# Attention sums of a chunk in one run over four PSUM banks, with the Exp table loaded by its own instruction

## The chip, the cores and the metric

The kernel runs on one core of one Trainium2 chip. Times are device microseconds (us) of that core, taken in several executions ("rounds") that alternate between the compared kernels on the same chip. The span is the time from the first to the last instruction in one profiled execution, and is some 1.7 us shorter than the time. The clock of a run is the share of full speed that TensorE was granted. Of the engines, TensorE is PE in the profile (its weight loads PEld), VectorE is DVE, ScalarE is ACT. A bracket at the end of a profile line gives how long the engine stood idle before it, and what ended that.

## The reference, cut to what matters

```python
xn  = layernorm(x)                      # x: 2048 x 512
q, k, v = split(xn @ wqkv)              # 32 heads of 16
# each position attends to itself and to 7 earlier ones, 2 apart
attn = softmax(einsum("bhsd,bhswd->bhsw", q, kg) * 16**-0.5)    # masked below 0
s = einsum("bhsw,bhswd->bhsd", attn, vg) @ wo
g = silu((gelu(xn @ w_gate) * (xn @ w_up)) @ w_down)            # inner width 1792
out = x + s * g
```

## The kernel before

The 2048 positions go in four chunks of 512. A chunk runs through a gate/up stage (14 groups: a `g_ps` and a `u_ps` of four 128x512 matmuls each), the projections of the next chunk (12 groups `qkv_ps`), and the down projection (`y_ps`, `s_ps`). Between these groups the attention of the chunk is laid in: VectorE multiplies q by k (`pk`) and the weights by v (`pv`), and TensorE sums these products over the head's elements or over the window with constant matrices of 32 columns, four such matmuls side by side. A list says ahead of which group each piece of attention stands.

The program lays out eight banks of 128x512 f32 in PSUM, the memory into which TensorE writes: five for the pool `mm`, through which all groups pass, two for the tile that is logits or half the sums in turn, one for the denominators. Tiles of one tag take turns in the same banks, so a new one waits until the last reader of the old one has ended.

```python
mm = pool("mm", 5, space=PSUM)
att = pool("att", 1, space=PSUM)

def logits(j):
    L = att.tile([P, WH, TQ], F32, name="L_ps", tag="pair")
    ...                                    # 32 matmuls of 32 columns
    nc.scalar.activation(out=E[:], in_=L[:], func=AF.Exp, scale=SCALE)

def denominators(j):
    den = att.tile([P, P], F32, name="den_ps")
    ...                                    # 8 matmuls with 32 columns of weights
    nc.vector.reciprocal(out=rs[:], in_=den[:])

def av_sums(j, gg):                        # one half: 16 matmuls
    o = att.tile([P, 2, TQ], F32, name="o_ps", tag="pair")
    for g in range(2):
        for wh in range(WH):
            for i in range(4):
                nc.tensor.matmul(o[H * i : H * (i + 1), g, :], lhsT=hsum[:],
                                 rhs=st[j]["pv"][2 * gg + g, wh][:, i, :],
                                 start=(wh == 0), stop=(wh == WH - 1))

# chunk 0, among the projections of chunk 1
at(("qkv", 1, 3), denominators, 0)
at(("qkv", 1, 3), av_sums, 0, 0)
at(("qkv", 1, 5), spread_reciprocals, 0)
at(("qkv", 1, 6), divide, 0, 0)
at(("qkv", 1, 10), av_sums, 0, 1)
at(("qkv", 1, 10), divide, 0, 1)
# chunks 1 to 3, among their own gate/up groups
at(("glu", j, 7), denominators, j)
at(("glu", j, 7), av_sums, j, 0)
at(("glu", j, 9), spread_reciprocals, j)
at(("glu", j, 9), divide, j, 0)
at(("glu", j, 12), av_sums, j, 1)
at(("glu", j, 12), divide, j, 1)

qs = [mm.tile([P, HQ], F32, name="qkv_ps", tag="mm") for _ in range(NC)]   # first q groups
```

The softmax here doesn't subtract the row's maximum and nothing guards it: scores larger than these inputs give would overflow.

Of the kernel before, what the change touches and what calls it, by code (L numbers as in the profile page):

```python
# [8 lines left out]
ALU = mybir.AluOpType  # L9
AF = mybir.ActivationFunctionType  # L10
BF16 = mybir.dt.bfloat16
F32 = mybir.dt.float32

P = 128
# [5 lines left out]
WH = 2  # L20
PAD = 16
TQ = 512
VW = TQ + WL * DIL
EPS = 1e-5
SCALE = DH ** -0.5
# [3 lines left out]
def kernel(  # L29
# [13 lines left out]
    nc = tc.nc  # L43
    B, S, D = A_x.shape
    DF = B_w_gate.shape[1]
    NT, NC, NF, NJ = S // P, D // P, DF // P, S // TQ
# [6 lines left out]
    def pool(name, bufs, **kw):  # L53
        return ctx.enter_context(tc.tile_pool(name=name, bufs=bufs, **kw))
# [10 lines left out]
    op = pool("op", 1)  # L65
# [1 line left out]
    sm2 = pool("sm2", 2)  # L67
    sm4 = pool("sm4", 4)
    dram = pool("dram", 1, space=bass.MemoryType.DRAM)
    mm = pool("mm", 5, space=bass.MemoryType.PSUM)  # L70
    att = pool("att", 1, space=bass.MemoryType.PSUM)


# [2 lines left out]
    wg_sb = wts.tile([P, NC, DF], BF16, name="wg_sb")  # L76
    wu_sb = wts.tile([P, NC, DF], BF16, name="wu_sb")
# [25 lines left out]
    def load_late_weights():  # L103
# [15 lines left out]
        out=vT.rearrange("(k p) n -> p k n", p=P)[:, :, 0:PAD],  # L119
        in_=warm[:, 0 : NC * PAD].rearrange("p (k n) -> p k n", k=NC),  # L120
# [39 lines left out]
    k_sb = big.tile([P, NC, PAD + S], BF16, name="k_sb")  # L160
# [78 lines left out]
    def project(ps, w, lo, j, i0=0, n=TQ, dks=range(NC)):  # L239
        for dk in dks:  # L240
            nc.tensor.matmul(  # L241
                ps[:],
                lhsT=w[:, dk, lo : lo + P],
                rhs=xnT[j][:, dk, i0 : i0 + n],
                start=(dk == 0),
                stop=(dk == NC - 1),
            )

    st = [dict(pk={}, pv={}) for _ in range(NJ)]

    def qkv(j, fo, i0=0, n=TQ, ps=None):
        which, c = divmod(fo, NC)
        if fo == 0 and i0 == 0:
            st[j]["q"] = qp.tile([P, NC, TQ], BF16, name="q_sb")
        if ps is None:
            ps = mm.tile([P, n], F32, name="qkv_ps", tag="mm")
            project(ps, wqkv_sb, fo * P, j, i0, n)
        if which == 0:
            nc.scalar.activation(out=st[j]["q"][:, c, i0 : i0 + n], in_=ps[:], func=AF.Copy)  # L259
        elif which == 1:  # L260
            lo = PAD + j * TQ + i0
            nc.scalar.activation(out=k_sb[:, c, lo : lo + n], in_=ps[:], func=AF.Copy)  # L262
        else:
            vst = sm4.tile([P, TQ], BF16, name="vst")
            nc.scalar.activation(out=vst[:], in_=ps[:], func=AF.Copy)  # L265
            lo = PAD + j * TQ
            nc.sync.dma_start(out=vT[c * P : (c + 1) * P, lo : lo + TQ], in_=vst[:])

# [21 lines left out]
        st[j]["pk"][w] = pk  # L290

    def logits(j):
        L = att.tile([P, WH, TQ], F32, name="L_ps", tag="pair")
        for wh in range(WH):
            for c in range(NC):
                for wl in range(WL):
                    nc.tensor.matmul(  # L297
                        L[H * wl : H * (wl + 1), wh, :],
                        lhsT=dsum[:, c, :],
                        rhs=st[j]["pk"][WL * wh + wl][:, c, :],  # L300
                        start=(c == 0),
                        stop=(c == NC - 1),
                    )
        E = st[j]["E"] = ep.tile([P, WH, TQ], BF16, name="E")
        nc.scalar.activation(out=E[:], in_=L[:], func=AF.Exp, scale=SCALE)
        if j == 0:
            for w in range(1, W):
                wh, wl = divmod(w, WL)
                nc.gpsimd.memset(E[H * wl : H * (wl + 1), wh, 0 : w * DIL], 0.0)

    def denominators(j):

        E = st[j]["E"]
        den = att.tile([P, P], F32, name="den_ps")
        for wh in range(WH):
            for q in range(4):
                nc.tensor.matmul(  # L317
                    den[H * q : H * (q + 1), :],
                    lhsT=hsum[:],
                    rhs=E[:, wh, q * P : (q + 1) * P],  # L320
                    start=(wh == 0),
                    stop=(wh == WH - 1),
                )
        rs = sm2.tile([P, P], BF16, name="rs")
        with nc.allow_low_precision(reason="as the softmax of the reference"):
            nc.vector.reciprocal(out=rs[:], in_=den[:])
        st[j]["rs"] = rs
# [20 lines left out]
        )  # L348
        st[j]["pv"][g, wh] = pv

    def av_sums(j, gg):

        o = att.tile([P, 2, TQ], F32, name="o_ps", tag="pair")
        for g in range(2):
            for wh in range(WH):
                for i in range(4):
                    nc.tensor.matmul(  # L357
                        o[H * i : H * (i + 1), g, :],
                        lhsT=hsum[:],
                        rhs=st[j]["pv"][2 * gg + g, wh][:, i, :],  # L360
                        start=(wh == 0),
                        stop=(wh == WH - 1),
                    )
        st[j]["o"] = o

    def divide(j, gg):
        if gg == 0:
            st[j]["oT"] = op.tile([P, NC, TQ], BF16, name="oT")
        nc.vector.tensor_tensor(  # L369
            out=st[j]["oT"][:, 2 * gg : 2 * gg + 2, :],  # L370
            in0=st[j]["o"][:],
            in1=st[j]["rb"][:].unsqueeze(1).to_broadcast([P, 2, TQ]),
            op=ALU.mult,
        )

    def glu(j, fc):
        g_ps = mm.tile([P, TQ], F32, name="g_ps", tag="mm")
        project(g_ps, wg_sb, fc * P, j)
        u_ps = mm.tile([P, TQ], F32, name="u_ps", tag="mm")
        project(u_ps, wu_sb, fc * P, j)  # L380
        ge = sm.tile([P, TQ], BF16, name="ge")
        nc.scalar.activation(out=ge[:], in_=g_ps[:], func=AF.Gelu_apprx_tanh)  # L382
        u = sm.tile([P, TQ], BF16, name="u")
        nc.scalar.activation(out=u[:], in_=u_ps[:], func=AF.Copy)  # L384
        h = hp.tile([P, TQ], BF16, name="h")
        nc.vector.tensor_tensor(out=h[:], in0=ge[:], in1=u[:], op=ALU.mult)  # L386
        st[j][fc] = h
# [35 lines left out]
    def at(key, fn, *args):  # L423
        side.setdefault(key, []).append((fn, args))
# [15 lines left out]
    for w in range(W):  # L440
        at(("glu", 0, w), qk_product, 0, w)
    at(("glu", 0, 9), logits, 0)
    for i in range(8):
        at(("glu", 0, 12 + i) if i < 2 else ("qkv", 1, (0, 1, 3, 4, 5, 6)[i - 2]),
           av_product, 0, i // 2, i % 2)
    at(("qkv", 1, 3), denominators, 0)
    at(("qkv", 1, 3), av_sums, 0, 0)
    at(("qkv", 1, 5), spread_reciprocals, 0)
    at(("qkv", 1, 6), divide, 0, 0)
    at(("qkv", 1, 10), av_sums, 0, 1)  # L450
    at(("qkv", 1, 10), divide, 0, 1)

    for j in range(1, NJ):
        for w in range(W):
            early = j > 1 and w < 3
            at(("qkv", j, 9 + w) if early else ("down", j - 1, w // 3), qk_product, j, w)
        for i in range(TPQ):
            at(("down", j - 1, i), load_v, j, [i])
        at(("glu", j, 0), logits, j)
        for i in range(8):  # L460
            at(("glu", j, 2 + i), av_product, j, i // 2, i % 2)
        at(("glu", j, 7), denominators, j)
        at(("glu", j, 7), av_sums, j, 0)
        at(("glu", j, 9), spread_reciprocals, j)
        at(("glu", j, 9), divide, j, 0)
        at(("glu", j, 12), av_sums, j, 1)
        at(("glu", j, 12), divide, j, 1)


    HT = TPQ // 2  # L470
    HQ = HT * P
# [11 lines left out]
    first_normalize(2)  # L483
    first_normalize(3)

    qs = [mm.tile([P, HQ], F32, name="qkv_ps", tag="mm") for _ in range(NC)]
    for dks in ((0, 1), (2, 3)):
        for fo in range(NC):
            project(qs[fo], wqkv_sb, fo * P, 0, 0, HQ, dks)
    for fo in range(NC):  # L490
        qkv(0, fo, 0, HQ, qs[fo])
    transpose(HT, copy=nc.vector.tensor_copy)
    for fo in range(NC, 2 * NC):
        qkv(0, fo, 0, HQ)
        if fo == NC:
            transpose(HT + 1, copy=nc.vector.tensor_copy)
# [3 lines left out]
    for fo in range(2 * NC):  # L500
        qkv(0, fo, HQ, HQ)
# [6 lines left out]
    for j in range(NJ):  # L508
        for fc in range(NF):
            run("glu", j, fc)  # L510
            glu(j, fc)
        if j + 1 < NJ:
            for i in range(12):
                run("qkv", j + 1, i)
                qkv(j + 1, i)
        for tt in range(TPQ):
            run("down", j, tt)
            down(j, tt)
# [28 lines left out]
```

## Time and profile before

| | before |
|---|---|
| time, median (first three runs) | 232.51 us (232.31 to 232.93) |
| span of the profiled run | 230.6 us |
| TensorE busy, clock granted | 97%, 0.998 |
| VectorE, ScalarE busy | 64%, 57% |
| matmuls | 1339 |

Most of the table says one thing: TensorE never rests. A reader then has to ask how much of its time is work. The busy share does not tell, since a matmul's modelled end overlaps the next one's start (a group of four is given as 1.03 us long, and the next starts after 0.86); the distance between starts does. The prediction shows the lines.

### The profile page before, as it was taken

The page shows a single profiled execution, that of the slowest core. Times are in us where ns is not written, and L with a number is a line of the kernel's source. Part 1 is how long each engine was busy: PE and PEld are TensorE (multiplying, and loading weights), DVE is VectorE, ACT ScalarE, POOL GpSimd, SP SyncE. Part 2 cuts the span into 40 slices and gives each one's busy share as a digit, 9 for nine tenths or more (in the row PEclk, how much of TensorE's full clock was granted, in tenths as well). Part 3 has the DMA queues.
Part 4 walks back from the last instruction along what each step waited for, and adds up shares of the span by engine and source line. Part 5 has one row for each costly group of instructions (what it writes and reads, how often), then busy time and mean ns, then how long its engine had stood idle before and what let it go on. Part 6 is the DMA issues. An engine that isn't in the chain of part 4 may idle for free.

```text
span 230.6 us, 3545 instructions
## 1 busy us (share of the span) xinstructions
PE 224.8 (97%) x1339; PEld 106.3 (46%) x1339; DVE 146.9 (64%) x234; ACT 132.3 (57%) x219; POOL 22.1 (10%) x61
## 2 busy tenths in 40 slices
PE   7999999999999999999999999999999999999994
PEld 5865444444444444444444444444444444444453
DVE  5593996897795198981677149951449429864132
ACT  4779869755414865756621595656741387576211
POOL 1058943000000000130000000000000000000000
PEclk9999999999999999999999999999999999999999
DMA  6999399921378211100277611000046810000001
GB/s 166 360 375 368 104 209 207 294 73 48 100 176 196 54 23 29 26 0 0 92 171 164 141 25 31 18 11 0 27 140 158 203 30 0 0 0 4 23 23 46
DMA packets 27057, 23.71 MB, mean 103 GB/s; under 512 B 6688, under 2 KB 27040, under 8 KB 27040
## 3 DMA queue, kind: packets, MB, share of 16 engines
q1 hardware_dynamic: 27040, 23.49, 38.8%
q8 instruction: 10, 0.16, 0.3%
q14 instruction: 7, 0.06, 0.1%
HBM read 18.22 MB, written 4.21 MB: 97 GB/s over the span
## 4 chain that ended last, share of the span: by engine, by line
PE 93%; DVE 3%; DMA 2%; SPq 1%; ACT 0%; issue 0%; DVEq 0%
PE g_ps L241 21%; PE y_ps L398 21%; PE u_ps L241 20%; PE qkv_ps L241 17%; PE s_ps L408 6%; PE L_ps L297 3%; PE o_ps L357 3%; DVE pv L343 2%; DMA wqkv_sb<-in_A_wqkv_dram 2%; SPq L83 1%; PE tr L207 1%; DVE h L386 0%; PE sp_ps L332 0%; PE den_ps L317 0%; ACT ge L382 0%
## 5 line engine op out<-in xcount | busy, mean ns | idle before, releaser
L241 PE MATMUL g_ps<-xnT,wg_sb 128*128 128x512 bf16 x224 | 57.6, 379 | 0.0
L241 PE MATMUL u_ps<-xnT,wu_sb 128*128 128x512 bf16 x224 | 57.5, 379 | 0.0
L398 PE MATMUL y_ps<-wd_sb,h 128*128 128x512 bf16 (+1 forms) x238 | 51.2, 367 | 0.0
L386 DVE TENSOR_TENSOR h<-ge,u 128x512 bf16<-128x512 bf16 x56 | 23.7, 424 | 34.1 <-ACT u L384 34.0
L287 DVE TENSOR_TENSOR pk<-q_sb,k_sb 128x2048 bf16<-128x2048 bf16 x32 | 37.8, 1220 | 11.6 <-ACT k_sb L262 11.6
L241 PE MATMUL qkv_ps<-xnT,wqkv_sb 128*128 128x512 bf16 (+1 forms) x224 | 43.0, 349 | 0.5 <-DMA wqkv_sb<-in_A_wqkv_dram 0.5
L382 ACT ACTIVATE ge<-g_ps 128x512 bf16<-128x512 f32 x56 | 33.6, 600 | 14.4 <-PE g_ps L241 12.9
L384 ACT ACTIVATE u<-u_ps 128x512 bf16<-128x512 f32 x56 | 33.6, 599 | 13.9 <-PE u_ps L241 13.9
L343 DVE TENSOR_TENSOR pv<-E,v_arr 128x2048 bf16<-128x2048 bf16 x32 | 38.6, 1217 | 0.0
L405 ACT ACTIVATE sl<-y_ps 128x512 bf16<-128x512 f32 (+1 forms) x17 | 9.7, 572 | 44.0 <-PE y_ps L398 44.0
L398 PEld LDWEIGHTS <-h 128*128 128x128 bf16 x238 | 23.3, 98 | 25.3
L241 PEld LDWEIGHTS <-wu_sb 128*128 128x128 bf16 x224 | 21.9, 98 | 26.6 <-issue 0.3
L241 PEld LDWEIGHTS <-wg_sb 128*128 128x128 bf16 x224 | 20.8, 98 | 26.7 <-issue 4.2
L241 PEld LDWEIGHTS <-wqkv_sb 128*128 128x128 bf16 x224 | 21.5, 98 | 20.0 <-DMA wqkv_sb<-in_A_wqkv_dram 0.7
L416 DVE TENSOR_TENSOR m<-s_ps,sl 128x512 bf16<-128x512 f32 (+1 forms) x17 | 11.2, 657 | 26.2 <-PE s_ps L408 26.2
L408 PE MATMUL s_ps<-wo_sb,oT 128*128 128x512 bf16 (+1 forms) x68 | 16.6, 366 | 0.0
L192 POOL TENSOR_TENSOR rstd<-rstd,mhalf 128x1 f32<-128x1 f32 x12 | 8.0, 665 | 79.4 <-DVE rstd L189 77.2
L259 ACT ACTIVATE q_sb<-qkv_ps 128x512 bf16<-128x512 f32 (+1 forms) x20 | 9.9, 513 | 5.4 <-PE qkv_ps L241 5.2
L265 ACT ACTIVATE vst<-qkv_ps 128x512 bf16<-128x512 f32 x16 | 9.6, 597 | 5.6 <-PE qkv_ps L241 5.6
L262 ACT ACTIVATE k_sb<-qkv_ps 128x512 bf16<-128x512 f32 (+1 forms) x20 | 10.2, 512 | 3.6 <-PE qkv_ps L241 3.2
L369 DVE TENSOR_TENSOR oT<-o_ps,rb 128x1024 bf16<-128x1024 f32 x8 | 9.7, 1218 | 1.4 <-PE o_ps L357 1.4
L408 PEld LDWEIGHTS <-oT 128*128 128x128 bf16 x68 | 6.6, 98 | 7.2
(49 smaller groups left out, 117.6 us busy)
## 6 DMA issues: line engine op xcount, KB each, us to landing
v_arr<-vT SPq DMA_DIRECT2D x16, 520.0 KB, 5.1
vT<-vst SPq DMA_DIRECT2D x16, 128.0 KB, 1.7
out_dram<-o_t SPq DMA_DIRECT2D x15, 128.0 KB, 2.3
wg_sb<-in_B_w_gate_dram SPq DMA_DIRECT2D x2, 896.0 KB
wu_sb<-in_B_w_up_dram SPq DMA_DIRECT2D x2, 896.0 KB, 13.7
wd_sb<-in_B_w_down_dram SPq DMA_DIRECT2D x1, 1792.0 KB, 16.8
wqkv_sb<-in_A_wqkv_dram SPq DMA_DIRECT2D x3, 512.0 KB, 5.1
x_sb<-in_A_x_dram SPq DMA_DIRECT2D x3, 512.0 KB, 9.7
```

The lines of the kernel that those rows point to most:

```text
L241: nc.tensor.matmul(ps[:], lhsT=w[:, dk, lo : lo + P], rhs=xnT[j][:, dk, i0 : i0 + n], start=(dk == 0), stop=(dk == NC - 1),)
L259: nc.scalar.activation(out=st[j]["q"][:, c, i0 : i0 + n], in_=ps[:], func=AF.Copy)
L262: nc.scalar.activation(out=k_sb[:, c, lo : lo + n], in_=ps[:], func=AF.Copy)
L287: nc.vector.tensor_tensor(out=pk[:], in0=st[j]["q"][:], in1=k_sb[:, :, off : off + TQ], op=ALU.mult)
L343: nc.vector.tensor_tensor(out=pv[:], in0=st[j]["E"][:, wh, :].unsqueeze(1).to_broadcast([P, 4, TQ]), in1=st[j]["va"][:, 4 * g : 4 * g + 4, ...
L369: nc.vector.tensor_tensor(out=st[j]["oT"][:, 2 * gg : 2 * gg + 2, :], in0=st[j]["o"][:], in1=st[j]["rb"][:].unsqueeze(1).to_broadcast([P, ...
L382: nc.scalar.activation(out=ge[:], in_=g_ps[:], func=AF.Gelu_apprx_tanh)
L384: nc.scalar.activation(out=u[:], in_=u_ps[:], func=AF.Copy)
L386: nc.vector.tensor_tensor(out=h[:], in0=ge[:], in1=u[:], op=ALU.mult)
L398: nc.tensor.matmul(y[:], lhsT=st[j][fc][:, tt * P : (tt + 1) * P], rhs=wd_sb[:, fc, cols], start=(fc == 0), stop=(fc == NF - 1),)
L408: nc.tensor.matmul(s[:], lhsT=st[j]["oT"][:, g, tt * P : (tt + 1) * P], rhs=wo_sb[:, g, cols], start=(g == 0), stop=(g == NC - 1),)
L416: nc.vector.tensor_tensor(out=m[:], in0=s[:], in1=sl[:, cols], op=ALU.mult)
```

## The change

Its intent: a chunk's 32 sums in one run, so that TensorE goes to the 32-column form and back less often. This needs four banks for the sums at once, so the pool `mm` falls from five to four, and the denominators move into the pool. The other parts are to make the smaller pool bearable: the Exp table is loaded by its own instruction ahead of the logits, and the four q groups at the start use the sums' banks, idle at that time. In chunk 0, where the sums waited for VectorE, the whole run and the spread of the reciprocals stand later.

```diff
-    mm = pool("mm", 5, space=bass.MemoryType.PSUM)
+    mm = pool("mm", 4, space=bass.MemoryType.PSUM)
...
     def logits(j):
-        L = att.tile([P, WH, TQ], F32, name="L_ps", tag="pair")
+        nc.scalar.preload_act_table(AF.Exp)
+        L = att.tile([P, NC, TQ], F32, name="L_ps", tag="quad")
...
-        den = att.tile([P, P], F32, name="den_ps")
+        den = mm.tile([P, P], F32, name="den_ps", tag="mm")
...
-    def av_sums(j, gg):
+    def av_sums(j):
-        o = att.tile([P, 2, TQ], F32, name="o_ps", tag="pair")
-        for g in range(2):
+        o = att.tile([P, NC, TQ], F32, name="o_ps", tag="quad")
+        for g in range(NC):
...
-    at(("qkv", 1, 3), av_sums, 0, 0)
-    at(("qkv", 1, 5), spread_reciprocals, 0)
-    at(("qkv", 1, 6), divide, 0, 0)
-    at(("qkv", 1, 10), av_sums, 0, 1)
-    at(("qkv", 1, 10), divide, 0, 1)
+    at(("qkv", 1, 8), spread_reciprocals, 0)
+    at(("qkv", 1, 10), av_sums, 0)
+    at(("qkv", 1, 10), divide, 0)
...
-        at(("glu", j, 7), denominators, j)
-        at(("glu", j, 7), av_sums, j, 0)
-        at(("glu", j, 9), spread_reciprocals, j)
-        at(("glu", j, 9), divide, j, 0)
-        at(("glu", j, 12), av_sums, j, 1)
-        at(("glu", j, 12), divide, j, 1)
+        at(("glu", j, 11), denominators, j)
+        at(("glu", j, 11), av_sums, j)
+        at(("glu", j, 12), spread_reciprocals, j)
+        at(("glu", j, 13), divide, j)
...
-    qs = [mm.tile([P, HQ], F32, name="qkv_ps", tag="mm") for _ in range(NC)]
+    q4 = att.tile([P, NC, TQ], F32, name="q4_ps", tag="quad")
+    qs = [q4[:, fo, 0:HQ] for fo in range(NC)]
```

More of the change, by code (lines that the diff above doesn't have):

```diff
@@ L241, in project @@
             nc.tensor.matmul(
-                ps[:],
+                ps,
                 lhsT=w[:, dk, lo : lo + P],
@@ L255, in qkv @@
         if ps is None:
-            ps = mm.tile([P, n], F32, name="qkv_ps", tag="mm")
+            ps = mm.tile([P, n], F32, name="qkv_ps", tag="mm")[:]
             project(ps, wqkv_sb, fo * P, j, i0, n)
         if which == 0:
-            nc.scalar.activation(out=st[j]["q"][:, c, i0 : i0 + n], in_=ps[:], func=AF.Copy)
+            nc.scalar.activation(out=st[j]["q"][:, c, i0 : i0 + n], in_=ps, func=AF.Copy)
         elif which == 1:
             lo = PAD + j * TQ + i0
-            nc.scalar.activation(out=k_sb[:, c, lo : lo + n], in_=ps[:], func=AF.Copy)
+            nc.scalar.activation(out=k_sb[:, c, lo : lo + n], in_=ps, func=AF.Copy)
         else:
             vst = sm4.tile([P, TQ], BF16, name="vst")
-            nc.scalar.activation(out=vst[:], in_=ps[:], func=AF.Copy)
+            nc.scalar.activation(out=vst[:], in_=ps, func=AF.Copy)
             lo = PAD + j * TQ
@@ L304, in logits @@
         E = st[j]["E"] = ep.tile([P, WH, TQ], BF16, name="E")
-        nc.scalar.activation(out=E[:], in_=L[:], func=AF.Exp, scale=SCALE)
+        nc.scalar.activation(out=E[:], in_=L[:, 0:WH, :], func=AF.Exp, scale=SCALE)
         if j == 0:
@@ L359, in av_sums @@
                         lhsT=hsum[:],
-                        rhs=st[j]["pv"][2 * gg + g, wh][:, i, :],
+                        rhs=st[j]["pv"][g, wh][:, i, :],
                         start=(wh == 0),
@@ L364, in av_sums, with divide @@
         st[j]["o"] = o
-    def divide(j, gg):
-        if gg == 0:
-            st[j]["oT"] = op.tile([P, NC, TQ], BF16, name="oT")
-        nc.vector.tensor_tensor(
-            out=st[j]["oT"][:, 2 * gg : 2 * gg + 2, :],
-            in0=st[j]["o"][:],
-            in1=st[j]["rb"][:].unsqueeze(1).to_broadcast([P, 2, TQ]),
-            op=ALU.mult,
-        )
+    def divide(j):
+        oT = st[j]["oT"] = op.tile([P, NC, TQ], BF16, name="oT")
+        for g in range(0, NC, 2):
+            nc.vector.tensor_tensor(
+                out=oT[:, g : g + 2, :],
+                in0=st[j]["o"][:, g : g + 2, :],
+                in1=st[j]["rb"][:].unsqueeze(1).to_broadcast([P, 2, TQ]),
+                op=ALU.mult,
+            )
     def glu(j, fc):
         g_ps = mm.tile([P, TQ], F32, name="g_ps", tag="mm")
-        project(g_ps, wg_sb, fc * P, j)
+        project(g_ps[:], wg_sb, fc * P, j)
         u_ps = mm.tile([P, TQ], F32, name="u_ps", tag="mm")
-        project(u_ps, wu_sb, fc * P, j)
+        project(u_ps[:], wu_sb, fc * P, j)
         ge = sm.tile([P, TQ], BF16, name="ge")
```

## The prediction

> **What bounds the kernel now.** I read the page first (busy shares, then the chain that ended last), then TensorE's timeline around each place that the change touches, then the timelines of ScalarE and VectorE in the same stretches.
>
> ```profile
> span 230.6 us, 3545 instructions
> PE 224.8 (97%) x1339; PEld 106.3 (46%) x1339; DVE 146.9 (64%) x234; ACT 132.3 (57%) x219; POOL 22.1 (10%) x61
> PEclk9999999999999999999999999999999999999999
> PE 93%; DVE 3%; DMA 2%; SPq 1%; ACT 0%; issue 0%; DVEq 0%
> ```
>
> TensorE (PE) is busy 97% of the span at full clock, and 93% of the chain is its own work, so the change must save time on PE. Busy is not peak, so I take starts: four 128x512 matmuls of one group start every 0.863 us (for example u_ps at 43.85, next group at 44.71), 0.216 us each. No part of the change removes a column from PE's stream (the order of instructions has 1339 matmuls before and after), so what can be won is only what stands between the groups: mode changes and stalls.
>
> Chunk 1, the second run of the attention sums (columns: start us, us, engine, line, op, count):
>
> ```profile
> 96.79 1.03 PE L241 MATMUL u_ps<-xnT,wu_sb 128*128 128x512 bf16 x4
> 97.75 1.05 PE L357 MATMUL o_ps<-pv,hsum 128*32 128x512 bf16 x16
> 98.73 1.04 PE L241 MATMUL g_ps<-xnT,wg_sb 128*128 128x512 bf16 x4
> ```
>
> u_ps should give way at 96.79 + 0.863 = 97.65; the 32-column matmuls start at 97.75, so going in costs 0.10. They are 16, four side by side: 4 x 0.216 = 0.863, end 98.61; g_ps starts at 98.73, so coming out costs 0.11. One visit of the sums costs 0.21 us beyond its work.
>
> Chunk 0, where the sums wait for a product on VectorE:
>
> ```profile
> 44.71 2.75 PE L241 MATMUL qkv_ps<-xnT,wqkv_sb 128*128 128x512 bf16 x12
> 47.40 0.29 PE L317 MATMUL den_ps<-E,hsum 128*32 128x128 bf16 x8
> 47.52 0.82 PE L357 MATMUL o_ps<-pv,hsum 128*32 128x512 bf16 x12
> 48.61 0.40 PE L357 MATMUL o_ps<-pv,hsum 128*32 128x512 bf16 x4 [0.27 <-DVE pv L343]
> 48.94 1.90 PE L241 MATMUL qkv_ps<-xnT,wqkv_sb 128*128 128x512 bf16 x8
> ```
>
> From den_ps to the next qkv_ps 1.54 us pass. In chunk 1 the same work, without a wait, takes 1.09 (den_ps at 87.70, g_ps at 88.79). The stall is 0.45 us; the bracket shows 0.27 because modelled ends hide the rest.
>
> Chunk 2, where the Exp table is loaded only after the logits have ended:
>
> ```profile
> 130.24 1.28 ACT L305 ACT_TABLE_LOAD   x1 [2.22 <-PE L_ps L297]
> 131.54 1.02 ACT L305 ACTIVATE E<-L_ps 128x1024 bf16<-128x1024 f32 x1
> 132.58 1.28 ACT L382 ACT_TABLE_LOAD   x1
> 133.87 0.60 ACT L382 ACTIVATE ge<-g_ps 128x512 bf16<-128x512 f32 x1
> ...
> 133.49 1.03 PE L241 MATMUL g_ps<-xnT,wg_sb 128*128 128x512 bf16 x4
> 134.52 1.02 PE L241 MATMUL u_ps<-xnT,wu_sb 128*128 128x512 bf16 x4
> ```
>
> The load waited for L_ps. In chunks 0, 1 and 3 it starts before the logits end (35.01, 73.52, 182.73). In chunk 2 everything behind it on ScalarE comes some 1.2 us later, and u_ps starts at 134.52 instead of 133.49 + 0.863 = 134.35: a stall of 0.17 until ge (ends 134.47) frees a bank, with all five in use. From this I take 0.05 us from an end on ScalarE to the start on PE.
>
> **What the Trainium skill says.** "TensorEngine Tiling (Array Packing)", Key Properties, says that changing the tiling mode drains TensorE; the trace agrees that a change costs, 0.10 going in and 0.11 coming out. "ScalarE: Activation LUTs", What ACT_TABLE_LOAD costs, gives 1283 ns for a load plus about 1380 ns of drain; the trace has 1283 ns, but no such drain beside it (load over at 131.52, Exp starts at 131.54), so I count 1.28. "PSUM — Partial Sum Buffer", PSUM bank collisions, tells one to guard by bank: a group can't write a bank until its reader has left it. The 0.17 us stall above is that. This is what a pool of four banks instead of five makes more likely.
>
> **The change part by part.** The order of instructions gives the new positions and what each waits for.
>
> 1. One run of sums in chunks 1 to 3. Before: den_ps + 16 matmuls after gate/up group 6, 16 more after group 11. After: den_ps + 32 matmuls after group 10. One visit fewer in each chunk: 3 x 0.21 = -0.63 us. Does it wait for the products? In chunk 1 the last product follows the h of group 8. That h starts 1.75 us after its u_ps, then 0.34, then 1.22 for the product. Without the earlier run group 8 has ended at 87.60 + 2 x 1.73 = 91.06, its u_ps began at 90.2, and the product is done at about 93.5. The sums start at 87.60 + 4 x 1.73 + 0.10 = 94.6 and need the last product 1.6 us later still. No wait. The spread one group later needs the reciprocal (0.95), hidden behind 1.7 us of sums and 1.7 of group 11.
>
> 2. Chunk 0. den_ps stays where it is, alone; all 32 sums stand at qkv 10. Visits: two before, two after, so nothing is saved in changes of mode. But the 0.45 us wait goes: the products end on VectorE at 53.91, and PE reaches the sums at about 47.62 + 20 x 0.216 + 0.22 (spread) + 8 x 0.216 = 53.9, needing the last product at the end of a 1.7 us run. -0.45 us. den_ps holds one of the four banks until the reciprocal at about 50.6; the compiled order shows the groups after it rotating over the other three, each free well before its turn (0.86 made, 0.60 to empty). No stall.
>
> 3. Exp table by its own instruction. In chunks 0, 1, 3 nothing moves: the load is already early. In chunk 2 it loses its wait, Exp starts at 130.2, and the 0.17 us stall goes. -0.17 us. The number of table loads stays 14.
>
> 4. Four banks instead of five. I take each group's bank from the compiled program and the end of its earlier reader from the trace. After Exp in chunk 1: g_ps wants to start at 78.97, its bank is free at 78.62 + 0.05, margin 0.3; chunk 0, 39.53 against 39.29, margin 0.24. These hold only because the table is early. One place doesn't hold, at the start of chunk 0's gate/up, where transposes share the pool:
>
> ```profile
> 20.73 1.03 PE L241 MATMUL u_ps<-xnT,wu_sb 128*128 128x512 bf16 x4
> ...
> 19.00 1.28 ACT L382 ACT_TABLE_LOAD   x1
> 20.30 0.60 ACT L382 ACTIVATE ge<-g_ps 128x512 bf16<-128x512 f32 x1
> ```
>
> This u_ps now takes the bank of the g_ps whose ge ends at 20.90: it starts at 20.95 instead of 20.73. +0.22 us. The transpose and groups after it then find their banks free.
>
> 5. First q groups in the sums' banks. They hold four banks that are idle then, so that the pool of four isn't empty. The four copies are now released by the last of 16 matmuls, so they start near 8.75 instead of 8.10; the k copy behind them ends at about 10.25, its bank is wanted at 10.31. 0 to +0.05 us.
>
> 6. VectorE does the same instructions. The division now comes as two of 1.22 us together, after the whole run. In chunk 0 that puts the next products about 0.6 us later; they ended at 70.1 where the logits took them at 73.7. In chunk 3, where no projections follow: the last h starts after both divisions, ending about 5.65 us after the start of group 12's g_ps; the down projection asks for it at 3.45 + 13 x 0.216 = 6.26. It holds, with 0.6 to spare.
>
> Sum: -0.63 - 0.45 - 0.17 + 0.22 = -1.03 us. The span of 230.6 becomes about 229.6 and the time of 232.51 about **231.5 us**, 0.4% faster.
>
> **Rivals.** (a) The smaller pool becomes the limit: PE waits for ScalarE after every Exp. The margins of 0.24 and 0.3 us are thin; if release takes 0.3 us longer than I read, each chunk loses some 0.1 to 0.3, the gain is eaten: 232.0 to 232.8. For it: the bank is the only resource that shrinks. Against: PE starts 0.05 us after the release in the one stall of this kind. (b) VectorE becomes the bound at the sums or at the end, with all eight products wanted at once and two divisions in a row ahead of the last h: up to 1 us lost, 232.3. Against: the margins above, and VectorE's 64%; in chunk 1 the moments of the next tiles also queue there, so the reciprocal may come late for the spread. (c) The change of mode is cheaper to avoid than I read: if the cost lies with the shape of the next weights rather than with the visit, den_ps alone in chunk 0 could cost more, and merging save less: 231.9. (d) The waits that go are only moved: chunk 0's missing stall returns at the later sums if the products slip. Then 231.9.
>
> **Range and chances.** The terms are each known to about 0.1 us; the four rivals are worth up to 1 us, all upwards. Nothing can win 2% (4.7 us), since all mode changes and stalls together are less. Two executions of the kernel before differ by up to 0.6 us. So 230.9 to 232.3, and within 2% almost surely.
>
> **What would show each step right or wrong.** In chunks 1 to 3 den_ps and 32 o_ps in one stretch of about 1.95 us from the first den_ps to the next g_ps (0.12 + 1.73 + 0.11), with no wait for pv. In chunk 0 no bracket at o_ps for pv, and den_ps followed by qkv_ps after about 0.23 us. In chunk 2 the Exp table load ahead of the end of L_ps, and no 0.17 gap at the third u_ps. At about 20.9 a late u_ps waiting for ge. Wrong would be: gaps on PE at the third g_ps after each Exp, at the spreads, or at the 14th matmul of the first down projection of chunk 3.

## The result, and the profile after

The changed kernel takes 231.61 us (median of 6, 231.38 to 231.72) against 232.58 for the kernel before (6 runs, 232.31 to 232.93). The ratio is 0.9956, 95% interval 0.9943 to 0.9968; like all ratios here it is the mean time of one kernel's fast runs over that of the other's that were recorded with them (three of these six are the three runs above), so not quite the ratio of the medians. The change gains 0.97 us of the medians, 0.4%, where 1.0 was forecast.

The page's first lines and the shares of the chain, after:

```profile
span 229.8 us, 3547 instructions
PE 224.7 (98%) x1339; PEld 107.6 (47%) x1339; DVE 147.5 (64%) x234; ACT 132.3 (58%) x219; POOL 20.9 (9%) x61
PE 95%; ACT 1%; DVE 1%; DMA 1%; issue 0%; DVEq 0%
```

The matmuls, their busy time and, within one point, the shares of the other engines are the same; what has gone is idle time and gaps on TensorE. TensorE's timeline in chunk 1 (start us, us, engine, line, op, count):

```profile
93.64 1.03 PE L241 MATMUL u_ps<-xnT,wu_sb 128*128 128x512 bf16 x4
94.59 0.29 PE L318 MATMUL den_ps<-E,hsum 128*32 128x128 bf16 x8
94.71 1.90 PE L358 MATMUL o_ps<-pv,hsum 128*32 128x512 bf16 x32
96.55 1.04 PE L241 MATMUL g_ps<-xnT,wg_sb 128*128 128x512 bf16 x4
```

One visit now: 0.09 going in (94.59 less 93.64 and 0.863), 0.12 for the denominators, 8 x 0.216 = 1.73 for the sums, 0.11 coming out. From den_ps to g_ps 1.96 us pass, where 1.95 was forecast. Chunk 0:

```profile
47.84 0.29 PE L318 MATMUL den_ps<-E,hsum 128*32 128x128 bf16 x8
48.07 4.49 PE L241 MATMUL qkv_ps<-xnT,wqkv_sb 128*128 128x512 bf16 x20
52.40 0.39 PE L333 MATMUL sp_ps<-rs,spread 128*128 128x128 bf16 x4
52.62 1.89 PE L241 MATMUL qkv_ps<-xnT,wqkv_sb 128*128 128x512 bf16 x8
54.44 1.91 PE L358 MATMUL o_ps<-pv,hsum 128*32 128x512 bf16 x32
56.28 1.90 PE L241 MATMUL qkv_ps<-xnT,wqkv_sb 128*128 128x512 bf16 x8
```

No bracket stands at o_ps: nothing waits for a product. ScalarE, then TensorE, in chunk 2:

```profile
127.81 1.28 ACT L293 ACT_TABLE_LOAD   x1
130.05 1.02 ACT L306 ACTIVATE E<-L_ps 128x1024 bf16<-128x1024 f32 x1 [0.96 <-PE L_ps L298]
...
133.26 1.03 PE L241 MATMUL g_ps<-xnT,wg_sb 128*128 128x512 bf16 x4
134.12 1.03 PE L241 MATMUL u_ps<-xnT,wu_sb 128*128 128x512 bf16 x4
```

The table load no longer waits; Exp is the one that waits for the logits, and the third u_ps follows its g_ps after 0.86. And the one new stall, on TensorE, with ScalarE's lines of the same time below:

```profile
20.11 1.03 PE L241 MATMUL g_ps<-xnT,wg_sb 128*128 128x512 bf16 x4
21.18 1.02 PE L241 MATMUL u_ps<-xnT,wu_sb 128*128 128x512 bf16 x4
...
19.24 1.28 ACT L383 ACT_TABLE_LOAD   x1
20.54 0.60 ACT L383 ACTIVATE ge<-g_ps 128x512 bf16<-128x512 f32 x1
```

u_ps starts 1.07 us after its g_ps instead of 0.86, 0.04 after ge has ended at 21.14.

**The sum by stretch.** The two profiled executions do not begin alike: TensorE's first q group starts at 6.80 before and at 7.06 after, because transposes and warm-up matmuls ahead of it ran slowly in the one and not in the other. Over all profiles that start lies between 6.80 and 7.76. So I compare from marks on TensorE, each the start of a group, which take the start-up out:

| stretch | before | after | difference | forecast |
|---|---|---|---|---|
| run of 60 projections (at 9.44; 9.68) to logits of chunk 0 | 24.79 | 24.99 | +0.20 | +0.22 (small pool) |
| to logits of chunk 1 | 39.44 | 38.98 | -0.46 | -0.45 (chunk 0's wait) |
| to logits of chunk 2 | 54.52 | 54.30 | -0.22 | -0.21 (one visit) |
| to logits of chunk 3 | 54.68 | 54.30 | -0.38 | -0.38 (one visit, Exp table) |
| to chunk 3's first y_ps | 28.53 | 28.31 | -0.22 | -0.21 (one visit) |
| sum | | | -1.08 | -1.03 |

I call "the steady part" of a run its span less the start of the run of 60 projections: 230.6 - 9.44 = 221.16 us before, 229.8 - 9.68 = 220.12 after, -1.04. Spans are rounded to 0.1, so it is good to some 0.1 us.

### The profile page after: what moved, and what is told of

It is laid out like the page before. It is cut to its first block, busy times and chain, and to the rows that moved or that the text cites. A ratio compares the mean times of both kernels' runs of the same rounds, so it can differ in the third digit from the quotient of the medians.

```text
span 229.8 us, 3547 instructions
## 1 busy us (share of the span) xinstructions
PE 224.7 (98%) x1339; PEld 107.6 (47%) x1339; DVE 147.5 (64%) x234; ACT 132.3 (58%) x219; POOL 20.9 (9%) x61
## 4 chain that ended last, share of the span: by engine, by line
PE 95%; ACT 1%; DVE 1%; DMA 1%; issue 0%; DVEq 0%
PE y_ps L399 21%; PE u_ps L241 21%; PE g_ps L241 21%; PE qkv_ps L241 17%; PE s_ps L409 6%; PE L_ps L298 3%; PE o_ps L358 3%; DMA x_sb<-in_A_x_dram 1%; PE tr L207 1%; PE q_ps L241 1%; DVE stats L176 1%; ACT L383 1%; PE den_ps L318 0%; PE sp_ps L333 0%; ACT xnT L216 0%; ACT ge L383 0%
## 5 line engine op out<-in xcount | busy, mean ns | idle before, releaser
L241 PE MATMUL qkv_ps<-xnT,wqkv_sb 128*128 128x512 bf16 (+1 forms) x208 | 41.1, 355 | 0.0
L259 ACT ACTIVATE q_sb<-qkv_ps 128x512 bf16<-128x512 f32 (+1 forms) x16 | 8.7, 544 | 3.6 <-PE qkv_ps L241 3.3
```

Source lines behind the costliest of these rows:

```text
L241: nc.tensor.matmul(ps, lhsT=w[:, dk, lo : lo + P], rhs=xnT[j][:, dk, i0 : i0 + n], start=(dk == 0), stop=(dk == NC - 1),)
```

## The experiments

The theory is that the gain is a sum of separate gaps on TensorE: 0.21 us for each visit to the 32-column form, 0.45 for a wait in chunk 0, 0.17 for a late table in chunk 2, less 0.21 for the smaller pool. Its main rivals are that the gaps at the visits are only modelled ends, that the waits won are given back, and that the smaller pool costs more than the margins told. Each experiment changes one part. They ran in three sets: the four below the changed kernel on one chip, the next four on another, and then the last two on that one. Of the eight runs of the kernel before that stand beside the last two, seven are those of the second set, some minutes earlier. Times are medians; "before" is the kernel before as recorded with them.

| run | time | before | ratio, 95% interval | steady part |
|---|---|---|---|---|
| changed kernel | 231.61 | 232.58 | 0.9956 (0.9943 to 0.9968) | 220.12 |
| e4_two_visits | 232.38 | 232.84 | 0.9990 (0.9972 to 1.0008) | 220.78 |
| e5_four_visits | 233.49 | 232.84 | 1.0031 (1.0014 to 1.0047) | 222.20 |
| e3_chunk0_early | 232.19 | 232.84 | 0.9994 (0.9959 to 1.0029) | 220.47 |
| e7_gelu_early | 231.35 | 232.84 | 0.9942 (0.9927 to 0.9957) | 219.89 |
| e2_no_preload | 233.24 | 232.74 | 1.0013 (0.9987 to 1.0038) | 221.13 |
| e6_four_banks_only | 233.85 | 232.74 | 1.0044 (1.0018 to 1.0070) | 222.21 |
| e1_preload_only | 232.52 | 232.74 | 0.9984 (0.9960 to 1.0008) | 220.93 |
| e9_q_in_pool | 231.61 | 232.74 | 0.9947 (0.9920 to 0.9974) | 220.11 |
| after_again | 232.09 | 232.71 | 0.9977 (0.9939 to 1.0015) | 220.07 |
| e8_one_visit_gelu_early | 231.05 | 232.71 | 0.9944 (0.9901 to 0.9986) | 219.63 |

All outputs are right. The times alone would leave the small differences open; the steady part and the lines decide. One run of `e3_chunk0_early` (233.86 us) had a mean clock of 0.993 and widens its interval; see the last experiment.

### Is a visit what costs?

The sums of chunks 1 to 3 are cut into two runs again (`e4_two_visits`), and into four (`e5_four_visits`):

```diff
 # in both, av_sums takes the list of sums to do (cut here); e4:
-        at(("glu", j, 11), av_sums, j)
+        at(("glu", j, 11), av_sums, j, (0, 1))
+        at(("glu", j, 12), av_sums, j, (2, 3))
```

> The changed kernel, but in chunks 1 to 3 the sums come in two visits again (denominators and 16 matmuls ahead of group 11, 16 ahead of group 12); all else as changed, four banks included. Theory (each visit costs about 0.21 us on TensorE, going in and coming out): 3 more visits, +0.63 us over the changed kernel, about 232.2 us, and each of the two runs shows 0.10 before and 0.11 after. Rival (the gaps at the visits are only modelled ends, and the gain came from the other parts): no slower than the changed kernel, 231.6.

> The changed kernel, but in chunks 1 to 3 the 32 sums come in four visits of 8 matmuls, ahead of groups 9, 10, 11 and 12. Theory: 9 more visits of 0.21 us, +1.9 us over the changed kernel, about 233.5, three times the loss of the kernel with two visits. Rival (no cost by visit): 231.6. A second rival (a cost by run that shrinks with shorter runs): between 232.2 and 233.5.

Against the changed kernel the steady part grows by 0.66 us with three more visits (0.63 expected) and by 2.08 with nine (1.9 expected). In the second, a visit of eight matmuls in chunk 1:

```profile
90.80 1.03 PE L241 MATMUL u_ps<-xnT,wu_sb 128*128 128x512 bf16 x4
91.75 0.61 PE L360 MATMUL o_ps<-pv,hsum 128*32 128x512 bf16 x8
92.30 1.04 PE L241 MATMUL g_ps<-xnT,wg_sb 128*128 128x512 bf16 x4
93.17 1.03 PE L241 MATMUL u_ps<-xnT,wu_sb 128*128 128x512 bf16 x4
```

It goes in at 91.75 instead of 91.66 (0.09), works 2 x 0.216 = 0.43, comes out at 92.30 instead of 92.18 (0.12), and the g_ps after it takes 0.87 instead of 0.863. That is about 0.22 a visit, the same for 8 matmuls as for 32: the cost is by visit, not by run length. Nine of them are 1.98. The remaining 0.1 is one wait: in chunk 1 the reciprocal, queued on VectorE behind the next tile's moments, ended at 99.61, and sp_ps started at 99.66 instead of about 99.55. Both rivals fall. What TensorE does in the 0.21 us is not shown by any run.

### Was chunk 0's wait worth its length?

`e3_chunk0_early` puts the first half of chunk 0's sums back where it was, with as many visits as the changed kernel has:

```diff
+    at(("qkv", 1, 3), av_sums, 0, (0, 1))
     at(("qkv", 1, 8), spread_reciprocals, 0)
-    at(("qkv", 1, 10), av_sums, 0)
+    at(("qkv", 1, 10), av_sums, 0, (2, 3))
```

> The changed kernel, but chunk 0's first half of the sums stands with the denominators at qkv 3 again. As many visits as in the changed kernel. Theory: the wait for the fourth product on VectorE is back, +0.45 us, about 232.05, with a bracket naming pv at o_ps near 49 us. Rival (the 0.45 us were won back by the free time that followed, the sums being ahead of nothing urgent): 231.6.

```profile
47.99 0.30 PE L318 MATMUL den_ps<-E,hsum 128*32 128x128 bf16 x8
48.11 0.82 PE L360 MATMUL o_ps<-pv,hsum 128*32 128x512 bf16 x12
49.18 0.40 PE L360 MATMUL o_ps<-pv,hsum 128*32 128x512 bf16 x4 [0.25 <-DVE pv L344]
49.51 4.49 PE L241 MATMUL qkv_ps<-xnT,wqkv_sb 128*128 128x512 bf16 x19
```

The wait is back: 1.52 us from den_ps to qkv_ps instead of 1.09, 0.43 lost; the steady part grows by 0.35 and the median by 0.58 against the changed kernel's (from another set of rounds). The rival, that such a wait is made good later, is out: from the run of 60 projections to chunk 3's second s_ps it takes 208.21 us (9.83 to 218.04) instead of 207.79 (9.68 to 217.47), so 0.42 is still missing there.

### What does the table instruction do, and what does the smaller pool cost?

`e2_no_preload` is the changed kernel without the instruction, `e1_preload_only` the kernel before with it, `e6_four_banks_only` the kernel before with four banks:

```diff
 e2:   def logits(j):
-          nc.scalar.preload_act_table(AF.Exp)
 e1:   def logits(j):
+          nc.scalar.preload_act_table(AF.Exp)
 e6:-  mm = pool("mm", 5, space=bass.MemoryType.PSUM)
    +  mm = pool("mm", 4, space=bass.MemoryType.PSUM)
```

> The changed kernel without the instruction that loads the Exp table ahead; the load comes before Exp by itself, and in chunk 2 it carries the wait for the logits again (the compiled order says so). Theory (with four banks the late table costs more than the 0.17 us that it cost with five, since already the third g_ps takes the bank of the first): a stall of about 1.03 us at chunk 2's third g_ps, about 232.6 us, all of the change's gain. Rival (the instruction is worth what it was worth before): +0.17, 231.8.

> The kernel before, with four banks in the pool instead of five and nothing else. Theory: +0.22 at the second u_ps of chunk 0, +0.86 more at chunk 2's third g_ps (1.03 in place of 0.17), and about 0.1 at the start, where the q groups hold the whole pool: +1.2 us over the kernel before, about 233.8. Rival (the fifth bank is not needed anywhere): 232.6.

> The kernel before, with the Exp table loaded ahead by its own instruction and nothing else. Theory: with five banks it is worth 0.17 us, about 232.4, and only chunk 2 changes. Rival (it lets Exp start earlier in each chunk and takes 1.28 us from ScalarE's queue in each): up to 4 x 0.17 and more, below 232.0.

`e2_no_preload`, chunk 2, ScalarE and then TensorE:

```profile
130.72 1.28 ACT L305 ACT_TABLE_LOAD   x1 [2.24 <-PE L_ps L297]
...
134.35 0.60 ACT L382 ACTIVATE ge<-g_ps 128x512 bf16<-128x512 f32 x1
...
133.08 1.03 PE L241 MATMUL u_ps<-xnT,wu_sb 128*128 128x512 bf16 x4
135.00 1.02 PE L241 MATMUL g_ps<-xnT,wg_sb 128*128 128x512 bf16 x4 [0.89 <-ACT ge L382]
```

The load waits for the logits again, and TensorE pays: the third g_ps starts 1.92 us after the u_ps before it instead of 0.86, a stall of 1.06. The bracket shows 0.89 of it. The steady part loses 1.01 us, all that the change gained. So one line is worth 1.0 us with four banks and little with five: added to the kernel before (`e1_preload_only`), it takes 0.23 off the steady part, 0.17 expected (chunk 2's third g_ps now starts at 133.89 and its u_ps at 134.75, 0.86 later), and the interval of the times reaches over 1. Its rival, a gain in every chunk, is out: in chunks 0, 1 and 3 the load had been early anyway, and it stands in the same place there. Why the compiled program made it wait in chunk 2 alone is not known.

`e6_four_banks_only` costs 1.05 in the steady part: 0.21 at the second u_ps of chunk 0, and in chunk 2 this:

```profile
133.56 1.03 PE L241 MATMUL u_ps<-xnT,wu_sb 128*128 128x512 bf16 x4
135.45 1.02 PE L241 MATMUL g_ps<-xnT,wg_sb 128*128 128x512 bf16 x4 [0.87 <-ACT ge L382]
```

a stall of 1.03 in place of 0.17. The 0.1 us expected at the start did not come: from the first q group to the run of 60 projections it takes 10.19 - 7.52 = 2.67 us, against 2.64 before.

The parts, each measured on its own, also add up: +1.05 for four banks, -1.01 for the table instruction with four banks, -0.66 for the visits and -0.42 for chunk 0's wait give -1.04, which is what the steady part lost.

### The q groups in the sums' banks

```diff
-    q4 = att.tile([P, NC, TQ], F32, name="q4_ps", tag="quad")
-    qs = [q4[:, fo, 0:HQ] for fo in range(NC)]
+    qs = [mm.tile([P, HQ], F32, name="qkv_ps", tag="mm")[:] for _ in range(NC)]
```

> The changed kernel with the first q groups in the pool's four banks again instead of the sums' banks. Theory: the third transpose waits for the first q copy and the groups after it for the others, 0.1 to 0.15 us in all, about 231.7. Rival (a pool with nothing free stops TensorE for each of four copies): 0.5 us or more, 232.1. Second rival (the copies are released one by one, so nothing is lost): 231.6.

My expectation was too high. From the first q group to the run of 60 projections 2.67 us pass, against 2.62 in the changed kernel: 0.05 us, and the times don't show it. The first bank becomes free just before the transpose wants it: the first q copy starts at 8.93 and takes some 0.39, the transpose starts at 9.38, and only the qkv_ps after it comes 0.04 late, at 9.64. This part of the change could be left out at next to no loss.

### The new stall, and a version that beats both

`e7_gelu_early` takes the new stall away by loading the Gelu table where ScalarE has slack, ahead of chunk 0's v copies:

```diff
+    nc.scalar.preload_act_table(AF.Gelu_apprx_tanh)
     for i in range(NC):
         run("qkv", 0, i)
```

> The changed kernel, with the Gelu table loaded by its own instruction ahead of chunk 0's v copies, where ScalarE has slack. Theory (the new stall of 0.21 us at the second u_ps of chunk 0 comes from the table load that stands between the g_ps and its Gelu, seen through four banks): the stall goes, -0.21 us, about 231.4; ge of the first group ends near 20 instead of 21.1, and the second u_ps follows its g_ps after 0.86. Rival (the stall comes from the pool alone, transposes and groups taking turns): the stall stays, 231.6, or moves to the v copies.

```profile
15.12 1.28 ACT L500 ACT_TABLE_LOAD   x1
16.41 1.58 ACT L265 ACTIVATE vst<-qkv_ps 128x512 bf16<-128x512 f32 x3
...
20.14 1.03 PE L241 MATMUL g_ps<-xnT,wg_sb 128*128 128x512 bf16 x4
21.00 1.03 PE L241 MATMUL u_ps<-xnT,wu_sb 128*128 128x512 bf16 x4
```

u_ps follows after 0.86. The three v copies queue behind the load (no idle time between them), but the fourth waits for TensorE again, so the queue is gone in time. The steady part is 0.23 shorter than the changed kernel's, 0.21 expected. The stall came from the table load seen through four banks; with the load elsewhere four banks are enough.

`e8_one_visit_gelu_early` also moves chunk 0's denominators into the run of its sums, so that chunk 0 too has one visit. It ran next to the changed kernel, unaltered (`after_again`):

```diff
-    at(("qkv", 1, 3), denominators, 0)
-    at(("qkv", 1, 8), spread_reciprocals, 0)
-    at(("qkv", 1, 10), av_sums, 0)
-    at(("qkv", 1, 10), divide, 0)
+    at(("qkv", 1, 9), denominators, 0)
+    at(("qkv", 1, 9), av_sums, 0)
+    at(("qkv", 1, 10), spread_reciprocals, 0)
+    at(("qkv", 1, 10), divide, 0)
```

> The changed kernel unaltered, on the same chip as the next one and as the kernel before. Theory: 1.0 us under the kernel before (232.5), about 231.5. Rival (the first comparison was helped by the chip): within 0.3 us of the kernel before.

> The changed kernel with the Gelu table loaded early in chunk 0, and chunk 0's denominators moved into the run of its sums (both at qkv 9, spread and division at qkv 10), so that chunk 0 too has one visit. Theory: -0.21 for the stall and -0.21 for the visit, 0.42 us under the changed kernel, about 231.2; den_ps directly ahead of 32 o_ps near 53 us, no wait for pv. Rival (VectorE: reciprocal and both divisions now come after the products, about 1.6 us later, and the next chunk's logits wait for their products): a gap ahead of L_ps near 73 us, 231.4 or more.

The steady part of `after_again` is 1.09 us under that of the kernel before, as in the first comparison (1.04). Its times gained less, 0.62 of the medians with an interval that reaches over 1: its q groups started at 7.69 in the profile, and one of its six runs, at 233.73 us, had a mean clock of 0.993. The profile of `e8_one_visit_gelu_early` (233.43 us, clock also 0.993) shows what such a run is:

```profile
7.76 3.53 PE L241 MATMUL q_ps<-xnT,wqkv_sb 128*128 128x256 bf16 x16 [1.37 <-DMA wqkv_sb<-in_A_wqkv_dram]
```

The weights came late, TensorE stood idle for 1.37 us, and the 16 matmuls of the first q groups then took 3.53 us instead of 1.92. From 7.70 to 11.30 the granted clock was 0.53; that costs 0.47 x 3.6 = 1.7 us, 0.7% of the span, which is the missing 0.007 of the mean clock. The late weights alone do not do it: `e5_four_visits` waited as long and went on at clock 1.00:

```profile
7.66 1.92 PE L241 MATMUL q_ps<-xnT,wqkv_sb 128*128 128x256 bf16 x16 [1.39 <-DMA wqkv_sb<-in_A_wqkv_dram]
```

Why the clock fell in the one and not in the other is left open. Past it, the steady part of `e8_one_visit_gelu_early` is 219.63 us, 0.44 under `after_again` (0.42 expected). Chunk 0 has one visit now:

```profile
55.20 0.30 PE L318 MATMUL den_ps<-E,hsum 128*32 128x128 bf16 x8
55.32 1.90 PE L358 MATMUL o_ps<-pv,hsum 128*32 128x512 bf16 x32
57.15 1.04 PE L241 MATMUL qkv_ps<-xnT,wqkv_sb 128*128 128x512 bf16 x3
```

There is no gap ahead of the next logits: s_ps at 74.66 in its profile, L_ps at 75.61, the usual 0.86 and 0.09. Its median of 231.05, with the slow start among its six runs, is the best here. The medians of the two are 1.04 apart, more than the 0.44 that the profiles show; where the rest lies is not shown: ahead of the 60 projections or in the rounds, which the timed runs don't tell apart.

## Why the prediction was right

- **The bound.** It was TensorE's stream, and only gaps in it counted. Each part moved the time by the gap that it opened or closed, and nothing else.
- **Step 1, visits.** -0.63 forecast; three stretches gave -0.22, -0.21 and -0.22, and putting the visits back cost 0.66. No run of sums waited for a product in chunks 1 to 3.
- **Step 2, chunk 0.** -0.45 forecast, -0.46 measured, 0.35 to 0.43 when undone.
- **Step 3, the Exp table.** -0.17 forecast; chunk 2's stretch gave -0.38, of which a visit is 0.21. Chunk 2's third u_ps follows its g_ps after 0.86 instead of 1.03, which is the 0.17. Right as a term of the sum, but it says too little: the prediction wrote that the margins "hold only because the table is early" and gave no number. With four banks the instruction is worth 1.0 us. Without it rival (a) would have come true, in one chunk of four: in `e2_no_preload` the other chunks show no stall after Exp.
- **Step 4, four banks.** +0.22 forecast at one place and nowhere else; 0.21 measured there, and no other stall. The margins of 0.24 and 0.3 us after Exp held.
- **Step 5, q groups.** 0 to +0.05 forecast. The four copies did start late, 1.94 us after the first q group (1.95 forecast), and cost nothing: 2.62 us to the run of 60 against 2.64.
- **Step 6, VectorE.** In chunk 3 the last h ended at 212.74, 5.64 us after group 12's g_ps (5.65 forecast), ahead of the matmul that wants it, the 14th of the y_ps that start at 210.56 (210.56 + 13 x 0.216 = 213.37).
- **The rivals.** (a) stayed away because of the table instruction. (b) VectorE did not become the bound: in chunk 1 the reciprocal, named as a risk, ended at 97.69, 0.6 us before its spread at 98.28. (c) is answered by the experiments with two and four visits, (d) by chunk 0's stretch and `e3_chunk0_early`.
- **The range** held for a reason that the prediction did not have right: it took 0.6 us as the spread between executions, and runs of the kernel before spread over 1.2 us (232.29 to 233.50). In the two profiles of the changed kernel such a difference lies in the start-up: spans 229.8 and 230.4, steady parts 220.12 and 220.07. For the timed runs it is not shown.
- **Luck.** That the medians differ by 0.97 us, so near the forecast, is partly luck: the second comparison gave 0.62. The evidence for the sum is the steady part, -1.04 and -1.09 against -1.03.

## What to carry to other kernels

When TensorE is the bound, measure the distances between starts of its groups, list every one that is longer than the work, and price a change by that list; past the start-up, 1 us of 232 was forecast to 0.1 in this way. The parts of such a change are not independent: here a table load placed early is worth 0.2 us with five banks and 1.0 with four, so before a buffer is taken away, look for whatever delays its release and move that first. And compare from a mark inside the program when the start-up varies by more than the change.

## What the Trainium skill lacked or had wrong

- "TensorEngine Tiling (Array Packing)", Key Properties, says that a change of mode drains TensorE and gives no price. Here it is 0.09 to 0.10 us going in and 0.11 to 0.12 coming out, the same for runs of 8, 16 and 32 matmuls.
- "ScalarE: Activation LUTs", What ACT_TABLE_LOAD costs, counts about 1380 ns of drain with each load of 1283 ns. The 1283 ns are right; between the end of the load and the Exp behind it the trace has 0.02 us, so a switch costs 1.3 us here, not 2.66.
- No page tells that a table load for which the kernel has no instruction of its own may carry the wait of the activation behind it. In chunk 2 it waited 2.22 us for the logits, which it does not read; in the other three chunks it did not.
- "TensorE: Matmul & The Clock Gate", Back-to-back issue gap, gives 131 ns a matmul as the sustained rate at N=512, and 216 for the isolated one. The sustained rate here is 216 ns: 48 projections in 10.36 us of the chain. The same page, Step-by-step: what each phase is for, has 215.7 ns for matmuls back to back, and that one holds.
- The same page, Why this matters for your kernels, warns of idle gaps of more than about 3 us. In one run here a gap of 1.37 us, after a start-up of small matmuls, was followed by 3.6 us at a granted clock of 0.53; in another a gap of 1.39 us was followed by clock 1.00. So the length of the gap alone does not decide.
